# Masked products, one joining product and two loads in other slots of a fused delta-rule and gated-MLP kernel

## The chip, the cores and the metric

The kernel runs on one core of one Trainium2 chip. The metric is the device time of one launch in microseconds (us), the median of the runs shown. The engines of the core are PE (TensorE, matrix products), DVE (VectorE), ACT (ScalarE), POOL (GpSimd) and SP (SyncE, which here issues every DMA). Each runs its own instructions in the order in which they stand in the program, and a semaphore holds an instruction back until what it needs is there.

## What is computed

An attention of the delta-rule kind, token by token, whose output rows go through a gated MLP. All tensors are float32; the batch is 4, with 8 heads, 768 tokens and a head size of 48, and the MLP has the widths 384 and 1536.

```python
k_n = k / (norm(k) + 1e-06)
for t in range(S):
    y[:, :, t] = einsum('bhd,bhde->bhe', q[:, :, t], state)
    v_old = einsum('bhde,bhd->bhe', state, kt)
    state = state + bt * einsum('bhd,bhe->bhde', kt, vt - v_old)
...
x = y.transpose(0, 2, 1, 3).reshape(B * S, H * D)
gate = 1.0 / (1.0 + np.exp(-(x @ w_gate)))
return (gate * (x @ w_val)) @ w_out
```

## The kernel before

**Groups.** The 768 tokens are cut into 12 groups of 64 (g = 0 to 11), each for all 32 heads at once. Inside a group the recurrence is solved as a triangular system, and between groups the state `su` is carried. A group passes these steps, each a function of its own: `gram` (K times K, tiles pg, and copies out of it), `norms` (the keys' norms, some 18 small DVE steps), `solve` or, for groups 0 to 2, `solve_halves` (the triangular inverse `mt`, on DVE), `masked` (K times Q, tiles pp, and its product with a mask on DVE, L324, into `kqp`), `rest` (what the state already predicts, pk, subtracted on DVE as R, L456), `updates` in three steps (U of the first 32 tokens, pu, L476, copied by ACT into `su`, L482; its effect on the others, pk again, L468; U of the other 32), `rows` (the output rows yy), `advance` (the state, pd) and `flip` (transposes to the MLP's layout).

`solve_halves` inverts two 16-by-16 halves with DVE and joins them with two products on PE: pz = A times mt (L413), then a transpose of mt into `scratch` on DVE (L421) and a copy of pz on ACT (L422), then pm (L424, the second joining product), and last mt minus pm on DVE (L429). It is a generator; each `steps(halves1)` runs it to its next `yield`.

**Slots.** The MLP of a group is 12 gate tiles (gv, L557 for group 0 and L560 for the others) and 12 output products (po, L585 and L591). They stand in slots: an even slot 2i issues gate tile i, an odd one the output product of the tile two before. 24 slots are a group. The attention of group g+1 is put into the slots of group g's MLP. In `slot(s)` the order is: the gate or output product; the functions in `plan[s]`; the halves of the gated tile (ACT's sigmoid L565, DVE's product L566, and the split into high and low part, L571 and L576, from group 1 on); the functions in `late[s]`; those in `tail[s]`. So the tables `plan`, `late` and `tail` are the order, written by hand. Only the small DVE steps of `norms`, `solve` and group 2's halves are dealt out by `spread`, which gives each slot a share of room 1.6 less `busy[s]`; a masked product counts 1.4 in its slot and the next.

**Weights.** 36 pieces of 384 KB come in as raw words. `scaled(n)` (two ACT steps, L189 and L191) makes piece n usable and, when done, issues the load of piece n + 6; DVE joins the words (L203, u), and ACT and DVE split them in high and low parts (w, L212 and L219) for the groups from 1 on. SP issues these loads in order with those of the groups: `load_rows` (kv, L117, part 1 the values and part 0 the keys by token, 384 KB each), `load_q` (kqp, L109, 2 x 256 KB) and `load_k` (L105).

**Banks.** The tiles pg, pz, pm, pp, pu, yy and pt share the two PSUM banks of the tag "aux" in turn: a tile waits until what read the one before the last is done.

Of the kernel before, what the change touches and what calls it, by code (L numbers as in the profile page):

```python
# [55 lines left out]
def deltanet_gated_mlp(ctx: ExitStack, tc: tile.TileContext, kd, qd, kv, beta, words, out):  # L56
# [29 lines left out]
    def pace(ins, after):  # L86
        if after is not None:
            tc.add_manual_dep(ins.ins, after.ins.name, mybir.DependencyInfo(mybir.DependencyClass.Sync, mybir.DependencyReason.DATA), reason="pace")
# [18 lines left out]
    def load_q(g, after=None):  # L107
        for e in range(2):
            ins = nc.sync.dma_start(kqp[g % 2][64 * e:64 * e + 64, 2 + e:4 + e].rearrange("p s c t -> p (s c t)"), qd[g, e])  # L109
            pace(ins, after)  # L110

    def load_rows(g, part):

        st = state[g]
        if "kv" not in st:
            st["kv"] = wk.tile([128, 2, CP, D], F32, name=f"kv_{g}", tag="kv", bufs=2)
        nc.sync.dma_start(st["kv"][:, part].rearrange("p c d -> p (c d)"), kv[g, :, part * CP * D:(part + 1) * CP * D])  # L117
        if part:
            st["beta"] = wk.tile([128, 32], F32, name=f"beta_{g}", tag="beta", bufs=2)
            nc.sync.dma_start(st["beta"], beta[:, g])  # L120

    def load_group(g):
        load_k(g)
        load_q(g)
        load_rows(g, 1)
        load_rows(g, 0)
# [57 lines left out]
    def scaled(n):  # L184

        half, lo, hi = words_of(n)
        nc.scalar.activation(lo.bitcast(I32), half, AF.Copy, bias=-4095.5 / 8192, scale=1 / 8192)  # L189
        h = hi.bitcast(F32)  # L190
        done[n] = nc.scalar.activation(h, h, AF.Prelu, scale=2.0 ** -112, alpha=-2.0 ** 32)  # L191
        if n + BEHIND in range(EAGER, len(pieces)):
            load_piece(n + BEHIND, done[n])
# [117 lines left out]
    def masked(g):  # L311

        kq = kqp[g % 2]
        pool, tag = (ps_aux, "aux") if g else (ps_out, "po")
        pp = [pool.tile([128, J, C], F32, name=f"pp_{g}_{e}", tag=tag) for e in range(2)]
        for j in range(J):
            for e, x in KINDS:
                r, t = 64 * e, tokens_at(e, x)
                nc.tensor.matmul(out=pp[e][t:t + 64, j], lhsT=kq[r:r + D, x, j], rhs=kq[r:r + D, 3 if x else 2 + 2 * e, j], start=True, stop=True)  # L319

        def masks():
            for e, x in sorted(KINDS):
                t, sec = tokens_at(e, x), 5 if x else 2 + 2 * e
                nc.vector.tensor_tensor(out=kq[t:t + 64, sec], in0=pp[e][t:t + 64],  # L324
                                        in1=pmask[t:t + 64, e].unsqueeze(1).to_broadcast([64, J, C]), op=ALU.mult)
                yield
        return masks()
# [105 lines left out]
    def rest(g):  # L433

        st = state[g]
        kq, V = kqp[g % 2], st["kv"][:, 1]
        st["pk"] = pk = [ps_seq.tile([128, J, D], F32, name=f"pk_{g}_{e}", tag="seq") for e in range(2)]
        if g == 0:
            for e in range(2):
                nc.tensor.matmul(out=pk[e].rearrange("q j d -> q (j d)"), lhsT=flat[:, 0:128], rhs=su[:, 2].rearrange("q j d -> q (j d)").bitcast(BF16)[:, 0:J * D],  # L440
                                 start=True, stop=True, skip_group_check=True)
        for j in range(J if g else 0):
            for e, x in KINDS:
                r, t = 64 * e, tokens_at(e, x)
                nc.tensor.matmul(out=pk[e][t:t + 64, j], lhsT=kq[r:r + D, x, j], rhs=su[r:r + D, 2 if x else e, j],  # L445
                                 start=j == 0, stop=True, skip_group_check=True)
        if g == 0:
            st["R"] = [V[:, e * J:(e + 1) * J] for e in range(2)]
        else:
            st["R"] = [wk.tile([128, J, D], F32, name=f"R_{g}_{e}", tag="row", bufs=3) for e in range(2)]  # L450
            less(g)
# [61 lines left out]
    def advance(g):  # L513

        if g == N - 1:
            return
        Kt = state[g]["kv"][:, 0]
        if 1:
            pd = [ps_seq.tile([128, J, D], F32, name=f"pd_{g}_{t}", tag="seq") for t in range(2)]
            for j in range(J):  # L520
                for e, x in KINDS:
                    r, t = 64 * e, tokens_at(e, x)
                    nc.tensor.matmul(out=pd[t // 64][r:r + D, j], lhsT=Kt[t:t + 64, e * J + j], rhs=su[t:t + 64, 3 if x else e, j], start=True, stop=True)  # L523
            for e, x in KINDS:
                r, t = 64 * e, tokens_at(e, x)
                sl = su[r:r + D, 2 if x else e]
                if g == 0:
                    nc.scalar.copy(sl, pd[t // 64][r:r + D])
                else:
                    nc.vector.tensor_tensor(out=sl, in0=sl, in1=pd[t // 64][r:r + D], op=ALU.add)  # L530
# [73 lines left out]
    plan = collections.defaultdict(list)  # L604
    late = collections.defaultdict(list)

    def steps(gen, n=1):
        def fn():
            for _ in range(n):
                next(gen, None)  # L610
        return fn

    def spread(gen, total, lo, hi, room=lambda s: 1.0, into=plan):

        done, upto, whole = 0, 0.0, sum(room(s) for s in range(lo, hi))
        for s in range(lo, hi):
            upto += total * room(s) / whole
            n = total if s == hi - 1 else round(upto)
            into[s].append(steps(gen, n - done))
            done = n  # L620
# [5 lines left out]
    def take(gen, n=1):  # L626
        for _ in range(n):
            next(gen, None)
# [37 lines left out]
    halves0, norms1, halves1 = solve_halves(0), norms(1), solve_halves(1)  # L666
# [32 lines left out]
    flip(0, 1)  # L699
    busy_array(gap[0], 2)  # L700
    tail = collections.defaultdict(list)
    for n, at in enumerate((0, 0, 1, 2, 3, 5, 6, 8, 9, 9, 10, 10, 11, 12, 12, 13, 14, 15, 16, 16, 17, 18, 18), 13):
        plan[at].append(lambda n=n: scaled(n))
    spread(joins, len(pieces) - 4, 0, 20)
    for at, n in ((0, 8), (1, 4), (2, 6), (3, 4), (4, 5), (5, 5), (6, 1), (9, 1), (10, 1), (11, 1)):
        plan[at].append(steps(halves1, n))
    plan[10].append(steps(halves1))
    spread(splits, 12, 9, 24, into=tail)
    spread(splits, 3, 24, 29, into=tail)
    spread(splits, len(pieces) + 1 - 15, 29, 44, into=tail)  # L710
    for s in range(4, 8):
        tail[s].append(steps(scalings[1], 4))
    for part in (1, 0):
        plan[6].append(lambda part=part: load_rows(2, part))
    plan[8].append(lambda: load_q(2))
    halves2 = solve_halves(2)
    plan[12].append(lambda: clear(2))
    plan[23].append(lambda: joint(2))
# [4 lines left out]
    def mask_later(g, s):  # L723
        def fn():
            masks = masked(g)
            take(masks, 2)
            plan[s + 1].insert(0, steps(masks, 2))
        late[s].append(fn)
        for i in range(2):
            busy[s + i] += 1.4  # L730

    def gram_later(g, s):
        def fn():
            copies = gram(g)
            for i, n in enumerate((4, 2, 4)):
                plan[s + 1 + i].append(steps(copies, n))
        late[s].append(fn)

    solves = []
    for g in range(N):  # L740
        w = W * (g - 1)
        if g == 0:
            late[3].append(lambda: advance(0))
            continue
        up, at_rows = (13, 19) if g < 3 else (10, 16)
        at_rest = {1: 8, 2: 28}.get(g, w + 6)
        late[at_rest].append(lambda g=g: rest(g))
        for step in range(3):
            late[w + up + 2 * step].append(lambda g=g, step=step: updates(g, step))
        late[w + at_rows].append(lambda g=g: rows(g))  # L750
        late[w + at_rows].append(lambda g=g: advance(g))
        for c in range(2):
            late[w + at_rows + 2].append(lambda g=g, c=c: flip(g, c))
            busy[w + at_rows + 2] += 0.6
        busy[at_rest] += 1.1
        busy[w + up + 2] += 1.1
        busy[w + at_rows] += 1.1
        busy[w + at_rows + 1] += 1.1
        if g == 1:
            mask_later(1, 11)  # L760
        else:
            if g > 2:
                plan[w - 27].append(lambda g=g: load_group(g))
            gram_later(g, {2: 3, 3: 32}.get(g, w - 18))
            mask_later(g, w + 1 if g == 2 else w - 12)
            if g > 2:
                solves.append((g, w - 13 if g == 3 else w - 14, w + 9))
            scaling(g, {2: 25, 3: 43}.get(g, w - 7))
# [77 lines left out]
```

## Time and profile before

| | us |
|---|---|
| median of the 3 runs | 649.55 |
| lowest and highest run | 645.4, 651.54 |
| the profiled execution's own time | 646.87 |
| its span, first to last instruction | 645.2 |
| granted clock of TensorE, mean | 0.994 |

The profile is one execution. A row of its timeline has the start and the length in us, the engine, the line, the operation, the tile written and the tiles read, the shapes, how many instructions are merged in it, and in brackets how long the engine stood idle before it and what ended that. Float32 products run as two instructions each, so a row of 64 matmuls is 32 in the program. In the DMA view a queue's row has its packets, megabytes, and the time that these took as a share of 16 engines; q1 carries the loads and stores that SP issues, q8 and q14 carry instructions. A slice is a fortieth of the span, 16.1 us.

### The profile page before, as it was taken

The page shows a single profiled execution, that of the slowest core. Times are in us where ns is not written, and L with a number is a line of the kernel's source. Part 1 is how long each engine was busy: PE and PEld are TensorE (multiplying, and loading weights), DVE is VectorE, ACT ScalarE, POOL GpSimd, SP SyncE. Part 2 cuts the span into 40 slices and gives each one's busy share as a digit, 9 for nine tenths or more (in the row PEclk, how much of TensorE's full clock was granted, in tenths as well). Part 3 has the DMA queues.
Part 4 walks back from the last instruction along what each step waited for, and adds up shares of the span by engine and source line. Part 5 has one row for each costly group of instructions (what it writes and reads, how often), then busy time and mean ns, then how long its engine had stood idle before and what let it go on. Part 6 is the DMA issues. An engine that isn't in the chain of part 4 may idle for free.

```text
span 645.2 us, 24064 instructions
## 1 busy us (share of the span) xinstructions
PE 622.1 (96%) x10548; PEld 582.1 (90%) x10556; DVE 467.3 (72%) x1443; ACT 320.6 (50%) x870; POOL 11.3 (2%) x30
## 2 busy tenths in 40 slices
PE   6789799999999999999999999999999999999996
PEld 4457578889999999999999999999999999999996
DVE  5878687688987977977977977977977977952221
ACT  4879584577345346246256256256255355334222
POOL 6000000000000000000000000000000000000000
PEclk9889999999999999999999999999999999999999
DMA  9595722202103102103102112112113100100101
GB/s 267 188 295 181 230 76 84 53 2 85 38 16 84 37 16 86 28 25 84 26 27 85 25 28 85 26 28 85 25 28 85 25 4 3 25 3 3 25 1 25
DMA packets 17769, 41.07 MB, mean 64 GB/s; under 512 B 4224, under 2 KB 7296, under 8 KB 17664
## 3 DMA queue, kind: packets, MB, share of 16 engines
q1 hardware_dynamic: 17664, 39.53, 21.3%
q8 instruction: 83, 1.36, 0.9%
q14 instruction: 22, 0.18, 0.1%
HBM read 34.80 MB, written 4.72 MB: 61 GB/s over the span
## 4 chain that ended last, share of the span: by engine, by line
PE 91%; DVE 4%; ACT 2%; issue 2%; DMA 1%; ACTq 0%; SPq 0%; DVEq 0%
PE gv L560 44%; PE po L591 23%; PE gv L557 3%; PE pu L476 3%; PE yy L502 2%; PE yy L505 2%; PE po L585 2%; PE pg L291 2%; PE pp L319 2%; PE pk L445 2%; PE pd L523 2%; PE pk L468 1%; PE pt L541 1%; PE pm L408 1%; PE pz L99 1%
## 5 line engine op out<-in xcount | busy, mean ns | idle before, releaser
L560 PE MATMUL gv<-xx,w 128*128 128x256 f32 x2376 | 307.5, 283 | 0.0
L560 PEld LDWEIGHTS gv<-xx,w 128*128 128x128 f32 x2376 | 301.3, 191 | 0.9
L591 PE MATMUL po<-w,h 128*128 128x384 f32 x792 | 166.2, 345 | 0.0
L565 ACT ACTIVATE sg<-gv 128x256 f32<-128x256 f32 x144 | 55.3, 384 | 203.6 <-PE gv L560 187.2
L591 PEld LDWEIGHTS po<-w,h 128*128 128x128 f32 x792 | 133.3, 188 | 3.1
L566 DVE TENSOR_TENSOR sg<-sg,gv 128x256 f32<-128x256 f32 x144 | 60.3, 419 | 78.0 <-ACT sg L565 77.5
L571 ACT CAST h<-sg 128x256 fp32r<-128x256 f32 x132 | 53.5, 405 | 51.5 <-DVE sg L566 50.2
L350 DVE TENSOR_TENSOR X<-X,tmp 128x126 f32<-128x126 f32 (+22 forms) x279 | 71.3, 256 | 9.0
L347 DVE TENSOR_TENSOR tmp<-X,gp 128x126 f32<-128x126 f32 (+22 forms) x279 | 71.0, 254 | 7.9
L576 DVE TENSOR_TENSOR h<-sg,h 128x256 fp32r<-128x256 f32 x132 | 55.0, 417 | 28.6 <-ACT h L571 28.6
L482 ACT COPY su<-pu 32x384 f32<-32x384 f32 x92 | 43.3, 471 | 15.1 <-PE pu L476 13.9
L279 ACT ACTIVATE kv<-kv,mq 128x48 f32<-128x48 f32 x192 | 48.2, 329 | 0.0
L324 DVE TENSOR_TENSOR kqp<-pp,pmask 64x512 f32<-64x512 f32 x48 | 32.2, 686 | 7.3 <-PE pp L319 6.3
L530 DVE TENSOR_TENSOR su<-su,pd 48x384 f32<-48x384 f32 x40 | 22.1, 552 | 19.3 <-PE pd L523 18.8
L303 ACT COPY G<-pg 32x256 f32<-32x256 f32 (+1 forms) x69 | 25.4, 368 | 18.1 <-PE pg L291 16.8
L557 PE MATMUL gv<-xx,u 128*128 128x256 f32 x144 | 33.7, 385 | 0.3 <-ACT xx L544 0.3
L557 PEld LDWEIGHTS gv<-xx,u 128*128 128x128 f32 x144 | 26.6, 190 | 4.9 <-ACT xx L544 0.8
L456 DVE TENSOR_TENSOR R<-kv,pk 128x384 f32<-128x384 f32 x44 | 22.4, 550 | 1.4 <-PE pk L445 1.4
L476 PEld LDWEIGHTS pu<-R,mt 32*32 32x32 f32 x1408 | 16.5, 105 | 4.9 <-issue 1.7
L212 ACT CAST w<-u 128x384 fp32r<-128x384 f32 x36 | 18.0, 508 | 5.7 <-DVE w L219 5.6
L476 PE MATMUL pu<-R,mt 32*32 32x48 f32 x1408 | 19.4, 202 | 0.9 <-DVE kqp L324 0.9
L189 ACT ACTIVATE raw<-raw 128x384 int32<-128x384 uint16 x36 | 19.9, 553 | 0.2 <-DMA raw<-in_words_dram 0.2
(104 smaller groups left out, 515.7 us busy)
## 6 DMA issues: line engine op xcount, KB each, us to landing
raw<-in_words_dram SPq DMA_DIRECT2D x36, 384.0 KB, 5.6
kv<-in_kv_dram SPq DMA_DIRECT2D x24, 384.0 KB, 4.3
kqp<-in_qd_dram SPq DMA_DIRECT2D x24, 256.0 KB, 4.2
kqp<-in_kd_dram SPq DMA_DIRECT2D x24, 192.0 KB, 3.5
out_dram<-ot SPq DMA_DIRECT2D x48, 96.0 KB, 2.2
beta<-in_beta_dram SPq DMA_DIRECT2D x12, 16.0 KB, 4.0
```

The lines of the kernel that those rows point to most:

```text
L279: nc.scalar.activation(V[:, c], V[:, c], AF.Copy, scale=mq[:, c, 0:1])
L347: nc.vector.tensor_tensor(out=tmp, in0=X[:, k:16, j:j + 1].to_broadcast([128, n, j]), in1=gp[:, j:j + 1, 0:j].to_broadcast([128, n, j]), o ...
L350: nc.vector.tensor_tensor(out=X[:, k:16, 0:j], in0=X[:, k:16, 0:j], in1=tmp, op=ALU.add)
L476: nc.tensor.matmul(out=pu[0 if g else x][r:r + 32, j], lhsT=mt[r:r + 32, e * J + j], rhs=R[e][r:r + 32, j], start=True, stop=True)
L482: nc.scalar.copy(su[r:r + 32, 3 if x else e], pu[0][r:r + 32])
L557: nc.tensor.matmul(out=pg[:, o], lhsT=parts[w, f][:, k * 128:(k + 1) * 128], rhs=x[0][:, k], start=k == 0, stop=k == KC - 1)
L560: nc.tensor.matmul(out=pg[:, o], lhsT=parts[w, f][:, a, k * 128:(k + 1) * 128], rhs=x[b][:, k], start=(k == 0 and q == 0), stop=(k == KC - ...
L565: nc.scalar.activation(h, st["gv", f][:, 0], AF.Sigmoid)
L566: nc.vector.tensor_tensor(out=h, in0=h, in1=st["gv", f][:, 1], op=ALU.mult)
L571: nc.scalar.copy(hh[:, 0], st["sg", f])
L576: nc.vector.tensor_tensor(out=hh[:, 1], in0=st["sg", f], in1=hh[:, 0].bitcast(F32), op=ALU.subtract)
L591: nc.tensor.matmul(out=po[s], lhsT=hh[:, a, ts], rhs=parts["o", f][:, w], start=(f == 0 and q == 0), stop=(f == NF - 1 and q == 2))
```

## The change

Four things move; no instruction is added or removed, and no size changes.

1. In the table of `scaled`, pieces 22 and 24 go from slots 9 and 10 to slots 10 and 11 (the table starts at piece 13).
2. In slot 10 the transpose L421 and the copy L422 of group 1 go to the front of `plan[10]`, and the second joining product goes from `plan[10]` to `late[10]`.
3. Part 0 of group 2's rows goes from slot 6 to slot 11, and group 2's q from slot 8 to slot 13.
4. The masked product of group 1 goes from `late[11]` to `late[14]`, that of group 3 from `late[36]` to `late[38]`. U of group 1 is in `late[13]` and `late[17]`, that of group 2 in `late[37]` and `late[41]`. The masks follow in the same slot and the next, and `busy` moves with them, so `spread` deals the small DVE steps differently around those slots.

```diff
-    for n, at in enumerate((0, 0, 1, 2, 3, 5, 6, 8, 9, 9, 10, 10, 11, 12, 12, 13, 14, 15, 16, 16, 17, 18, 18), 13):
+    for n, at in enumerate((0, 0, 1, 2, 3, 5, 6, 8, 9, 10, 10, 11, 11, 12, 12, 13, 14, 15, 16, 16, 17, 18, 18), 13):
         plan[at].append(lambda n=n: scaled(n))
...
-    for at, n in ((0, 8), (1, 4), (2, 6), (3, 4), (4, 5), (5, 5), (6, 1), (9, 1), (10, 1), (11, 1)):
+    for at, n in ((0, 8), (1, 4), (2, 6), (3, 4), (4, 5), (5, 5), (6, 1), (9, 1), (11, 1)):
         plan[at].append(steps(halves1, n))
-    plan[10].append(steps(halves1))
+    plan[10].insert(0, steps(halves1))
+    late[10].append(steps(halves1))
...
-        plan[6].append(lambda part=part: load_rows(2, part))
-    plan[8].append(lambda: load_q(2))
+        plan[{1: 6, 0: 11}[part]].append(lambda part=part: load_rows(2, part))
+    plan[13].append(lambda: load_q(2))
...
-            mask_later(1, 11)
+            mask_later(1, 14)
...
-            mask_later(g, w + 1 if g == 2 else w - 12)
+            mask_later(g, {2: 25, 3: 38}.get(g, w - 12))
```

On PE, slots 10 to 14 stood like this before (pm_1 is the second joining product, pp_1 the masked product, whose 32 rows alternate between two banks; pu_1_0 is the first U, also 32 rows):

```order
L557 MATMUL gv_0_5_1189<-xx_0_781,u_7_1013 128x256 x6
L408 MATMUL pm_1_1112<-scratch_86 32x32 x64
L585 MATMUL po_0_0_979<-u_6_987,sg_0_3_1025 128x384
L585 MATMUL po_0_1_980<-u_6_987,sg_0_3_1025 128x384
L319 MATMUL pp_1_0_1293<-kqp1_77 64x64
L319 MATMUL pp_1_1_1294<-kqp1_77 64x64
...
L557 MATMUL gv_0_6_1329<-xx_0_781,u_8_1035 128x256 x3
L557 MATMUL gv_0_6_1329<-xx_0_781,u_9_1108 128x256 x3
L585 MATMUL po_0_0_979<-u_8_1035,sg_0_4_1057 128x384
L585 MATMUL po_0_1_980<-u_8_1035,sg_0_4_1057 128x384
L476 MATMUL pu_1_0_0_1370<-R_1_0_1094,mt_78 32x48
```

and now stand like this, on PE up to slot 14:

```order
L408 MATMUL pm_1_1105<-scratch_86 32x32 x64
L585 MATMUL po_0_0_979<-u_6_987,sg_0_3_1024 128x384
L585 MATMUL po_0_1_980<-u_6_987,sg_0_3_1024 128x384
L557 MATMUL gv_0_6_1294<-xx_0_781,u_8_1034 128x256 x3
L557 MATMUL gv_0_6_1294<-xx_0_781,u_9_1101 128x256 x3
L585 MATMUL po_0_0_979<-u_8_1034,sg_0_4_1054 128x384
L585 MATMUL po_0_1_980<-u_8_1034,sg_0_4_1054 128x384
L476 MATMUL pu_1_0_0_1343<-R_1_0_1091,mt_78 32x48
...
L557 MATMUL gv_0_7_1383<-xx_0_781,u_10_1199 128x256 x6
L319 MATMUL pp_1_0_1401<-kqp1_77 64x64
L319 MATMUL pp_1_1_1402<-kqp1_77 64x64
```

The masked product has passed the gate tile gv_0_6, an output product, the first U and the gate tile gv_0_7; the second joining product already stood behind gv_0_5 on PE.

On SP, the loads from group 2's values on stood in this order before (kv_2 are group 2's rows, kqp0 from in_qd its q, raw the weight pieces):

```order
L117 DMA kv_2_1016<-in_kv_dram 128x768
L120 DMA beta_2_1018<-in_beta_dram 128x32
L117 DMA kv_2_1016<-in_kv_dram 128x768
L172 DMA raw_26_1050<-in_words_dram 128x768
L109 DMA kqp0_76<-in_qd_dram 64x1024 x2
L172 DMA raw_27_1102<-in_words_dram 128x768
L172 DMA raw_28_1106<-in_words_dram 128x768
```

and on SP they are now, from the six pieces that follow beta_2 on:

```order
L120 DMA beta_2_1018<-in_beta_dram 128x32
L172 DMA raw_26_1049<-in_words_dram 128x768
L172 DMA raw_27_1099<-in_words_dram 128x768
L172 DMA raw_28_1193<-in_words_dram 128x768
L172 DMA raw_29_1197<-in_words_dram 128x768
L172 DMA raw_30_1280<-in_words_dram 128x768
L172 DMA raw_31_1284<-in_words_dram 128x768
L117 DMA kv_2_1016<-in_kv_dram 128x768
L172 DMA raw_32_1303<-in_words_dram 128x768
L172 DMA raw_33_1307<-in_words_dram 128x768
L172 DMA raw_34_1333<-in_words_dram 128x768
L109 DMA kqp0_76<-in_qd_dram 64x1024 x2
```

The keys of group 2 have passed six weight pieces and its q eight.

On DVE, slots 36 and 37 had this order before (L253 is a norm step of group 3, h_1_5 and sg_1_6 are halves of gated tiles, pp_3 the masked product of group 3):

```order
L253 SCALAR_TENSOR_TENSOR ny_3_2260<-nt_3_2261,ny_3_2260 128x32
L576 TENSOR_TENSOR h_1_5_2272<-sg_1_5_2242,h_1_5_2272 128x256
L566 TENSOR_TENSOR sg_1_6_2298<-sg_1_6_2298,gv_1_6_2277 128x256
L324 TENSOR_TENSOR kqp1_77<-pp_3_0_2301,pmask_81 64x512 x2
L219 TENSOR_TENSOR w_24_2275<-u_12_1347,w_24_2275 128x384
L219 TENSOR_TENSOR w_25_2338<-u_12_1347,w_25_2338 128x384
L324 TENSOR_TENSOR kqp1_77<-pp_3_1_2302,pmask_81 64x512 x2
```

and has this one now, on DVE in slot 36:

```order
L253 SCALAR_TENSOR_TENSOR ny_3_2260<-nt_3_2261,ny_3_2260 128x32
L249 SCALAR_TENSOR_TENSOR nt_3_2261<-ny_3_2260 128x32
L251 TENSOR_TENSOR nt_3_2261<-nt_3_2261,gp_3_2257 128x32
L253 SCALAR_TENSOR_TENSOR ny_3_2260<-nt_3_2261,ny_3_2260 128x32
L255 TENSOR_TENSOR ns_3_2262<-ny_3_2260,gp_3_2257 128x32
L576 TENSOR_TENSOR h_1_5_2272<-sg_1_5_2242,h_1_5_2272 128x256
L566 TENSOR_TENSOR sg_1_6_2302<-sg_1_6_2302,gv_1_6_2277 128x256
L219 TENSOR_TENSOR w_24_2275<-u_12_1310,w_24_2275 128x384
```

Four norm steps now stand ahead of the gated tile's halves, and the masks (L324) have gone two slots down. ACT's order in those slots is unchanged: the cast L571 of h_1_6, then the four copies L482 of U.

## The prediction

> **What bounds the kernel now.** I read the page first, for the share of each engine over the span and for the slices.
>
> ```profile
> span 645.2 us, 24064 instructions
> PE 622.1 (96%) x10548; PEld 582.1 (90%) x10556; DVE 467.3 (72%) x1443; ACT 320.6 (50%) x870; POOL 11.3 (2%) x30
> PE   6789799999999999999999999999999999999996
> q8 instruction: 83, 1.36, 0.9%
> ```
>
> TensorE (PE) works 96% of the span. From the sixth slice on each is at 90% or more, so what can be given back lies in the first five (16 us each) and, in small pieces, behind them. The view of waits, for PE alone, says what the holes are (total us, times, longest):
>
> ```profile
> PE pg L291 <- DMA kqp<-in_kd_dram: 4.3, 2, 3.8
> PE pp L319 <- issue: 2.9, 1, 2.9
> PE pu L476 <- issue: 2.5, 2, 1.5
> PE pz L99 <- DVE tmp L391: 2.3, 1, 2.3
> PE pu L476 <- DVE kqp L324: 0.9, 1, 0.9
> PE pm L408 <- issue: 0.8, 2, 0.6
> ```
>
> The first, third and fourth lie before 40 us, where the change does nothing. The change reaches the second (the masked product of group 1), the fifth (group 2's U behind group 3's masked product) and the last (the joining product pm of group 1). "issue" means that no semaphore explains the wait. The timeline of PE around the two large ones:
>
> ```profile
> 64.17 1.47 PE L408 MATMUL pz<-mt,scratch 32*32 32x32 f32 x128
> 65.57 2.86 PE L557 MATMUL gv<-xx,u 128*128 128x256 f32 x12
> 68.73 0.31 PE L408 MATMUL pm<-scratch 32*32 32x32 f32 x12 [0.30 <-DVE nt L249]
> 69.59 1.19 PE L408 MATMUL pm<-scratch 32*32 32x32 f32 x116 [0.55 <-issue]
> 70.71 1.56 PE L585 MATMUL po<-u,sg 128*128 128x384 f32 x4
> 72.20 0.34 PE L319 MATMUL pp<-kqp 48*64 48x64 f32 x7
> 75.45 1.08 PE L319 MATMUL pp<-kqp 48*64 48x64 f32 x57 [2.92 <-issue]
> 76.47 2.86 PE L557 MATMUL gv<-xx,u 128*128 128x256 f32 x12
> 79.16 1.45 PE L585 MATMUL po<-u,sg 128*128 128x384 f32 x4
> ```
>
> Both "issue" waits fall inside a run of equal matmuls, and between them lie 116 + 4 + 7 = 127. The page gives instruction queue q8 83 packets, 1.36 MB, so 16.4 KB each; PE's 10,548 + 10,556 instructions over 83 are 254, or 127 matmuls with their weight loads. So I read these waits as PE out of instructions until its next packet comes. The DMA view in three stretches, 66.7 to 66.9, then 67 to 73, then 73 to 73.1 us:
>
> ```profile
> q8 instruction: 1, 0.02, 43.2%
> ...
> q1 hardware_dynamic: 657, 1.84, 100.2%
> ...
> q8 instruction: 1, 0.02, 68.3%
> ```
>
> One packet begins at 66.8 and PE resumes at 69.59; none begins from 67 to 73 while the load queue keeps all 16 engines at 100.2%; the next begins at 73.0 and PE resumes at 75.45. From a packet's start to PE's restart it is 2.4 to 2.8 us. [...]
>
> **The change, part by part.** *The second joining product and its inputs.* On PE, pm already stood behind its slot's gate tile, so that order stays. What moves is ahead of it: the transpose L421 on DVE passes two joins, the copy L422 on ACT passes raw_22 and raw_23 (and raw_24 goes a slot later). pm waited 0.30 us for them; now both end before the gate tile does (65.57 + 2.86 = 68.43). Gain 0.30; if not, 0.
>
> *The masked product of group 1.* Its 64 matmuls leave slot 11 and come after slot 14's gate tile. PE then runs pm from 68.43 (128 matmuls, 1.24 at the rate of the 116), po (72.20 - 70.71 = 1.49), and the gate tile gv(0,6) from 71.16. The place where the packet is needed, 127 to 128 matmuls behind the twelfth of pm, becomes the eighth of gv(0,6), at 71.16 + 7 x 0.224 (2.69 us for 12, from 76.47 to 79.16) = 72.73. If the packet still let PE go at 75.45, 2.72 us of wait would stay, and 1.46 us would be gained in all: PE would have done seven gate matmuls (1.57) more by then than before, and seven of pp (0.11) less.
>
> *The loads.* What must shorten the rest is the queue of loads. SP's order before, from the timeline of its issues:
>
> ```profile
> 60.16 0.42 SPq L117 DMA_DIRECT2D kv<-in_kv_dram  x1
> 63.45 0.33 SPq L172 DMA_DIRECT2D raw<-in_words_dram  x1
> 63.82 1.11 SPq L109 DMA_DIRECT2D kqp<-in_qd_dram  x2
> 65.03 7.54 SPq L172 DMA_DIRECT2D raw<-in_words_dram  x7
> ```
>
> The kv load (384 KB) goes behind raw_31 and the two q loads (512 KB) behind raw_34, past six and eight weight pieces. 0.90 MB leave the queue ahead of the packet at 73.0. At the 1.84 MB in 6 us of the stretch above this is 2.9 us, so the packet would begin at 70.1 and PE could go on at 72.5 to 72.9, against a need at 72.73. The bounds: nothing (2.72 stays) and all. I take all, because raw_28 and raw_30 also go a slot later, and the packet before it, which cost 0.55 us, loses a kv load ahead of it too. Together the three waits are 0.30 + 0.55 + 2.92 = 3.77 us.
>
> What covers the moved work? Rows of DVE, of PE's U in slot 17, and of ACT:
>
> ```profile
> 70.83 0.69 DVE L429 TENSOR_TENSOR mt<-mt,pm 128x512 f32<-128x512 f32 x1
> 76.56 2.70 DVE L324 TENSOR_TENSOR kqp<-pp,pmask 64x512 f32<-64x512 f32 x4 [5.04 <-PE pp L319]
> 87.43 1.01 DVE L456 TENSOR_TENSOR R<-kv,pk 128x384 f32<-128x384 f32 x2
> 90.33 0.88 PE L476 MATMUL pu<-R,mt 32*32 32x48 f32 x64
> 79.36 0.38 ACT L565 ACTIVATE sg<-gv 128x256 f32<-128x256 f32 x1 [7.15 <-PE gv L557]
> ```
>
> DVE stood idle 5.04 us and ACT 7.15 us for the late PE, so both can follow an earlier PE. The new order puts the masks (2.70 us) ahead of R's second difference, for which slot 17's U waits. From L429's end (71.5) to R's end (88.4) DVE now has 11.9 us of work; with 0.6 us of norm and solve steps that come earlier and about 1.4 us of waiting for the gate of slot 14, R ends near 85.3. U would start at 90.33 - 3.77 = 86.6. About 1 us is left. pp's second bank is now the one that U used, free when four copies L482 (1.96 us) are done; a whole gate tile (2.69) lies between. Cost 0; without that cover, 1 to 2 us.
>
> *The masked product of group 3.* It goes from slot 36 behind slot 38's gate tile, so that U no longer waits for its bank.
>
> ```profile
> 135.87 1.41 PE L319 MATMUL pp<-kqp 48*64 48x64 f32 x64
> 137.21 1.32 PE L591 MATMUL po<-w,h 128*128 128x384 f32 x6
> 139.41 0.88 PE L476 MATMUL pu<-R,mt 32*32 32x48 f32 x64 [0.88 <-DVE kqp L324]
> 140.22 2.41 PE L560 MATMUL gv<-xx,w 128*128 128x256 f32 x18
> 143.62 0.58 PE L468 MATMUL pk<-su,L 32*32 32x48 f32 x35
> 137.43 0.41 DVE L566 TENSOR_TENSOR sg<-sg,gv 128x256 f32<-128x256 f32 x1
> 138.04 0.41 ACT L571 CAST h<-sg 128x256 fp32r<-128x256 f32 x1
> 140.35 1.96 ACT L482 COPY su<-pu 32x384 f32<-32x384 f32 x4 [1.91 <-PE pu L476]
> 142.71 0.22 DVE L255 TENSOR_TENSOR ns<-ny,gp 128x32 f32<-128x32 f32 x1
> ```
>
> Here something is late next. The planner fills the room with four norm steps (some 0.95 us by their spacing) ahead of DVE's sg(1,6), which then ends at 138.8 instead of 137.84. ACT's cast L571 waits for it, and the copies L482 stand behind that cast: 139.2 + 1.96 = 141.2. PE without pp and the wait does po from 135.87 (about 1.1 to the next start), U from 136.95 (0.81 to 140.22 before) and the gate tile until 140.0. pp's second bank is U's, so pp waits 1.2 us. The gain: pk started at 143.62 and would start at 140.0 + 1.2 + 1.1 + 1.1 = 143.4. I take 0.2; bounds: the whole 0.9 and the quarter that pp took over the 1.1 of group 1's, and a loss of 0.5 if the cast is later still.
>
> Sum: 3.77 + 0.2 = 3.97 us. The profiled execution took 646.87 (span 645.2 and 1.7 around it), so 642.9.
>
> **The rivals.** *The packet comes no sooner.* Gain 1.46 + 0.2: 645.2 us. For it: no view shows when a packet is asked for, which may have been at 72. [...]
>
> *The waits are no refills and stay.* Only 0.30 + 0.2 is gained: 646.4 us. Against it stands the count of 127.
>
> *A refill is late in the new dense place, and it ends slower.* Counting 128 on from gv(0,6)'s eighth, the next two packets are needed in the 44th matmul of pp and the 24th of slot 17's U; between the two places only about 6.9 us pass (the rest of pp, po, pk, the gate tile, po, a third of U), and the kv and q loads now run there. With the 2.8 us from a packet's start to PE's restart, the packet may begin 4.1 us after the first place. To end slower it must begin 4.1 + 3.97 = 8.1 us after it; the one at 73.0 began 3.4 after the wait of 69.59. The loads there (0.90 MB moved, raw_35 and the next k, 0.79 MB) are 5.5 us at the rate above, so they alone don't do it; twice that, 11 us, would wait 6.9 us and give 642.9 + 6.9 = 649.8.
>
> *More goes than this trace shows.* The runs of before spread from 645.4 to 651.54 us. If part of that is the length of these waits, other runs gain more; with the lowest run as base, 645.4 - 3.97 = 641.4.
>
> **How the numbers follow.** The three runs have the median 649.55, 2.7 above the profiled one. If those 2.7 us lie elsewhere, the median after is 649.55 - 3.97 = 645.6; if they lie in waits that go, 642.9. I forecast the middle, 644.2. Chances: the forecast 0.62, no sooner 0.17, waits stay 0.08, slower 0.04, more goes 0.09. The range goes from 641.4 to 648.0, the latter being the second case on the median run (649.55 - 1.66 = 647.9); it leaves the third and fourth on such a run outside. About 1% is what a measurement of this kernel can tell; faster by that is below 643.05: the last case and a third of the first, 0.29. Slower by 1% needs 656, which only the dense place with several late refills could give, 0.03. The rest, 0.68, is within 1%.
>
> **What would show it.** Right: no "issue" wait of PE between 60 and 90 us; a q8 packet that begins before 71 us; L319 of group 1 between slot 14's gate tile and po; a wait of pp in slot 38 on L482 of about a microsecond, and none of U in slot 37. Wrong: a wait inside gv(0,6) (loads were not what delayed the packet), one inside pp, pk or U of slots 14 to 17 (dense refills), or one of slot 17's U on L456 (masks ahead of R).

## The result and the profile after

| | before | after |
|---|---|---|
| median of the runs, us | 647.71 (11 runs) | 642.88 (11 runs) |
| lowest and highest, us | 644.94, 651.54 | 641.85, 644.45 |
| ratio of after to before, 95% interval | | 0.9928 [0.9906, 0.9949] |

The change makes the kernel 4.8 us faster, 0.7%, against a forecast of 644.2 us. One execution of the changed kernel, the first and profiled one, took 1505.85 us, with matmuls 1.4 to 2.3 times as long by shape, for a cause that no run shows; the median counts it (642.83 without), the lowest and highest leave it out, and the profile shown here is that of a second job of the same kernel (e1 below), whose own time is 642.67 us. Its page, by the same lines as before:

```profile
span 640.9 us, 24065 instructions
PE 620.9 (97%) x10548; PEld 581.4 (91%) x10556; DVE 467.3 (73%) x1443; ACT 320.7 (50%) x870; POOL 11.3 (2%) x30
PE   6789999999999999999999999999999999999996
q8 instruction: 83, 1.36, 0.9%
```

The work is the same (10,548 matmuls, 83 instruction packets), and the fifth slice has gone from 7 to 9. The view of waits, for PE (total us, times, longest):

```profile
PE pg L291 <- DMA kqp<-in_kd_dram: 4.7, 2, 4.1
PE pu L476 <- issue: 1.7, 2, 1.0
PE pz L99 <- DVE tmp L391: 1.4, 1, 1.4
PE pp L319 <- ACT su L482: 0.8, 1, 0.8
PE pm L408 <- issue: 0.7, 2, 0.5
PE gv L557 <- issue: 0.5, 1, 0.5
PE yy L502 <- ACT su L482: 0.4, 1, 0.4
```

The 2.9 us of pp on "issue" are gone, and so are the 0.9 us of pu on L324. Three waits are new: 0.5 us inside a gate tile, and two on L482, ACT's copies of U. (The waits of pu lie before 40 us, and the longer one of pm is now in group 2's pm, behind the part that was changed.) The timeline of PE in slots 10 to 17 shows the first:

```profile
66.58 1.29 PE L408 MATMUL pm<-scratch 32*32 32x32 f32 x128
67.80 1.56 PE L585 MATMUL po<-u,sg 128*128 128x384 f32 x4
69.19 1.89 PE L557 MATMUL gv<-xx,u 128*128 128x256 f32 x8
71.63 1.13 PE L557 MATMUL gv<-xx,u 128*128 128x256 f32 x4 [0.55 <-issue]
72.60 1.45 PE L585 MATMUL po<-u,sg 128*128 128x384 f32 x4
73.99 0.88 PE L476 MATMUL pu<-R,mt 32*32 32x48 f32 x64
74.80 2.86 PE L557 MATMUL gv<-xx,u 128*128 128x256 f32 x12
77.59 1.16 PE L319 MATMUL pp<-kqp 48*64 48x64 f32 x64
...
85.06 0.88 PE L476 MATMUL pu<-R,mt 32*32 32x48 f32 x64
```

pm runs through with no wait. PE stops once, behind eight matmuls of gv(0,6); to within one matmul that is where the prediction put the place at which the next packet is needed. Neither pp nor slot 17's U waits. (Group 0's first gate tile starts at 42.31 us here and at 43.90 before. This start lies between 41.65 and 44.51 us in the profiles of this study, earlier or later for kernels that are alike up to there, so times below are counted from it.)

The other two waits stand in slots 38 and 43. First PE, then ACT (e1 again):

```profile
131.93 0.88 PE L476 MATMUL pu<-R,mt 32*32 32x48 f32 x64
132.74 2.40 PE L560 MATMUL gv<-xx,w 128*128 128x256 f32 x18
135.08 0.33 PE L319 MATMUL pp<-kqp 48*64 48x64 f32 x2
136.24 1.15 PE L319 MATMUL pp<-kqp 48*64 48x64 f32 x62 [0.84 <-ACT su L482]
146.99 0.31 PE L502 MATMUL yy<-su,kqp 48*64 48x48 f32 x2
147.68 1.14 PE L502 MATMUL yy<-su,kqp 48*64 48x48 f32 x62 [0.37 <-ACT su L482]
```

```profile
133.84 0.41 ACT L571 CAST h<-sg 128x256 fp32r<-128x256 f32 x1 [0.70 <-DVE sg L566]
134.27 1.92 ACT L482 COPY su<-pu 32x384 f32<-32x384 f32 x4
145.27 0.41 ACT L571 CAST h<-sg 128x256 fp32r<-128x256 f32 x1 [1.56 <-DVE sg L566]
145.71 1.92 ACT L482 COPY su<-pu 32x384 f32<-32x384 f32 x4
```

U ends at 132.8, but its copies begin only at 134.27: ACT stands idle at the cast ahead of them, which waits for DVE. The copies end at 136.2, and pp, whose second bank they free, goes on at 136.24. The same happens 11 us later with U's other half: copies until 147.6, the row products yy from 147.68.

To see where the time went, PE's timeline is cut at four starts: group 0's first gate tile, pm of slot 10, the first state product pd (L523) behind it, and PE's matmul 2,900 (counted from 0), which lies behind slot 43. The last column is a stretch within the third part: from slot 36's gate tile, gv(1,6), to the pd that follows. The profiled executions of all kernels that are told of below (us; the rest to the last matmul was 477.2 before, 477.2 under e1 and 477.1 under e9):

| kernel | to pm | pm to pd | pd to matmul 2,900 | gv(1,6) to pd |
|---|---|---|---|---|
| before | 24.83 | 28.63 | 65.10 | 20.56 |
| after (e1) | 24.28 | 25.51 | 65.99 | 21.19 |
| after (e9) | 24.28 | 25.03 | 65.59 | 21.20 |
| e2, the loads alone | 24.85 | 28.87 | 65.01 | 20.57 |
| e3, group 1's masked product alone | 24.85 | 26.79 | 65.12 | 20.57 |
| e4, group 3's masked product alone | 24.83 | 32.01 | 65.72 | 21.19 |
| e12, after without parts 1 and 2 | 24.85 | 24.99 | 65.54 | 21.19 |
| e7, after without part 3 | 24.52 | 26.16 | 65.88 | 21.19 |
| e6 and e11, after without group 3's move | 24.28, 24.28 | 25.58, 25.46 | 64.98, 64.66 | 20.56, 20.56 |
| e5 and e10, after with the copies first | 24.28, 24.28 | 25.37, 25.75 | 63.69, 63.96 | 19.41, 19.41 |

So the change gains 0.55 us in the first part and 3.1 to 3.6 in the second, and loses 0.5 to 0.9 in the third: 2.8 to 3.7 us in all, while the medians differ by 4.8. The last column makes the third part sharper: the move of group 3's masked product costs 0.63 us in each trace that has it. What else differs there lies ahead of slot 36, above all the "issue" wait of group 2's pm (0.28 us before, 0.54 under e1, none under e9). The experiments ask which part of the change does what, whether the "issue" waits are refills, and where the rest of the 4.8 us is.

### The profile page after: what moved, and what is told of

It is laid out like the page before. It is cut to its first block, busy times and chain, and to the rows that moved or that the text cites. A ratio compares the mean times of both kernels' runs of the same rounds, so it can differ in the third digit from the quotient of the medians.

```text
span 1504.0 us, 24073 instructions
## 1 busy us (share of the span) xinstructions
PE 1494.8 (99%) x10556; PEld 1296.0 (86%) x10556; DVE 476.7 (32%) x1443; ACT 322.6 (21%) x870; POOL 11.2 (1%) x30
## 4 chain that ended last, share of the span: by engine, by line
PE 99%; DMA 0%; ACT 0%; SPq 0%; issue 0%
PE gv L560 47%; PE po L591 24%; PE gv L557 6%; PE pu L476 3%; PE po L585 3%; PE pp L319 2%; PE pg L291 2%; PE yy L505 2%; PE yy L502 2%; PE pk L445 2%; PE pt L541 1%; PE pk L468 1%; PE pd L523 1%; PE gap L99 1%; PE pz L99 1%; PE pm L408 0%
## 5 line engine op out<-in xcount | busy, mean ns | idle before, releaser
L560 PEld LDWEIGHTS gv<-xx,w 128*128 128x128 f32 x2376 | 715.0, 423 | 42.4 <-issue 23.0
L560 PE MATMUL gv<-xx,w 128*128 128x256 f32 x2376 | 735.1, 531 | 0.0
L591 PE MATMUL po<-w,h 128*128 128x384 f32 x792 | 384.8, 680 | 0.0
L591 PEld LDWEIGHTS po<-w,h 128*128 128x128 f32 x792 | 269.3, 370 | 41.3 <-issue 24.7
L557 PE MATMUL gv<-xx,u 128*128 128x256 f32 x144 | 87.8, 830 | 0.0
L557 PEld LDWEIGHTS gv<-xx,u 128*128 128x128 f32 x144 | 50.8, 358 | 32.8 <-issue 30.3
L571 ACT CAST h<-sg 128x256 fp32r<-128x256 f32 x132 | 53.3, 404 | 29.5 <-DVE sg L566 28.7
L482 ACT COPY su<-pu 32x384 f32<-32x384 f32 x92 | 43.2, 469 | 49.5 <-PE pu L476 48.3
L585 PE MATMUL po<-u,sg 128*128 128x384 f32 x48 | 45.0, 1129 | 0.0
L476 PE MATMUL pu<-R,mt 32*32 32x48 f32 x1408 | 42.3, 325 | 0.0
L324 DVE TENSOR_TENSOR kqp<-pp,pmask 64x512 f32<-64x512 f32 x48 | 32.3, 687 | 19.4 <-PE pp L319 19.0
L291 PE MATMUL pg<-kqp 48*64 48x64 f32 x768 | 32.1, 377 | 4.5 <-DMA kqp<-in_kd_dram 4.5
L291 PEld LDWEIGHTS pg<-kqp 48*64 48x64 f32 x768 | 30.4, 290 | 6.0 <-DMA kqp<-in_kd_dram 4.6
```

What stands on the lines that cost most here:

```text
L291: nc.tensor.matmul(out=pg[e][t:t + 64, j], lhsT=kq[r:r + D, x, j], rhs=kq[r:r + D, x, j], start=True, stop=True)
L476: nc.tensor.matmul(out=pu[0 if g else x][r:r + 32, j], lhsT=mt[r:r + 32, e * J + j], rhs=R[e][r:r + 32, j], start=True, stop=True)
L557: nc.tensor.matmul(out=pg[:, o], lhsT=parts[w, f][:, k * 128:(k + 1) * 128], rhs=x[0][:, k], start=k == 0, stop=k == KC - 1)
L560: nc.tensor.matmul(out=pg[:, o], lhsT=parts[w, f][:, a, k * 128:(k + 1) * 128], rhs=x[b][:, k], start=(k == 0 and q == 0), stop=(k == KC - ...
L571: nc.scalar.copy(hh[:, 0], st["sg", f])
L585: nc.tensor.matmul(out=po[s], lhsT=st["sg", f][:, s * 128:(s + 1) * 128], rhs=parts["o", f], start=f == 0, stop=f == NF - 1)
```

## The experiments

Three jobs, each with runs of the kernel before on its chip: the median of before was 647.91 us with e1 to e4 (29 runs, 644.44 to 651.74), 647.08 with e5 to e8 (14 runs) and 647.41 with e9 to e12 (11 runs). Ratios are to before.

**e1: the changed kernel once more.**

> The changed kernel as it is, for an undisturbed profile. Theory (late instruction packets): no wait of PE named issue between 60 and 90 us, a q8 packet beginning before 71 us, pp of group 3 waiting about 1.2 us in slot 38 on U's copies L482; time 4 to 5 us under the kernel before. Rival (the packet comes no sooner): a wait of 2 to 3 us inside the gate tile gv(0,6). Rival (no refills): the waits stand at the masked product of group 1, in slot 14.

Measured: 642.82 us (642.16 to 643.96), ratio 0.9918 [0.9898, 0.9939].

**e2: the loads alone, on the kernel before.**

```diff
-        plan[6].append(lambda part=part: load_rows(2, part))
-    plan[8].append(lambda: load_q(2))
+        plan[{1: 6, 0: 11}[part]].append(lambda part=part: load_rows(2, part))
+    plan[13].append(lambda: load_q(2))
```

> The kernel before with only the two loads in later slots (kv part 0 in slot 11, q in slot 13). Theory (the packet stands behind the loads): the wait of 2.92 us at the eighth pp shrinks to under 0.8 us and the 0.55 goes, so 2.5 to 3.4 us faster. Rival (loads are not what delays the packet): the wait stays at 2.5 to 3 us and the time within 0.5 us of before.

Measured: 643.76 us, ratio 0.9952 [0.9928, 0.9977]; nine of the 12 runs lie between 642.93 and 644.85, two at 648.3 and 648.5. The profiled execution took 646.38. Its PE timeline:

```profile
67.53 1.50 PE L408 MATMUL pm<-scratch 32*32 32x32 f32 x128 [0.51 <-DVE nt L249]
...
72.89 1.48 PE L319 MATMUL pp<-kqp 48*64 48x64 f32 x57 [2.09 <-issue]
74.30 4.07 PE L557 MATMUL gv<-xx,u 128*128 128x256 f32 x12
```

Of the 0.55 us inside pm no wait is listed any more (its 128 matmuls take 1.50 us here and 1.29 under e1), but of the 2.92 us 2.09 are left, where hardly 0.8 were expected. The packet began 27.8 us behind the first gate tile, and 29.1 before: 1.3 us sooner, not 2.9. And the gate tile takes 4.07 us instead of 2.86: the granted clock is 0.50 from 73.4 to 76.8 us.

**e3: group 1's masked product alone, on the kernel before.**

```diff
-            mask_later(1, 11)
+            mask_later(1, 14)
```

> The kernel before with only group 1's masked product in slot 14. Theory: the packet still begins at about 73 us, so a wait of about 2.7 us stands now inside gv(0,6), at its seventh to ninth matmul, and the time is about 1.5 us under before. Rival (no refill, something in the masked product): the wait goes to slot 14 with it or vanishes, which would give 3 us.

Measured: 644.07 us, ratio 0.9948 [0.9927, 0.997]. The profiled execution (643.65):

```profile
68.17 1.19 PE L408 MATMUL pm<-scratch 32*32 32x32 f32 x116 [0.64 <-issue]
70.68 1.89 PE L557 MATMUL gv<-xx,u 128*128 128x256 f32 x8
73.54 1.13 PE L557 MATMUL gv<-xx,u 128*128 128x256 f32 x4 [0.97 <-issue]
```

The wait stands behind the eighth matmul of gv(0,6) and is 0.97 us long, where about 2.7 were expected; pm's waits, which that figure took as gone, stay in e3 (0.29 and 0.64 us). The packet began 28.8 us behind the first gate tile, hardly sooner than before; what shrank the wait is that PE has gate matmuls to do until then, as the first rival says. From pm to pd this alone gains 1.84 us.

**e4: group 3's masked product alone, on the kernel before.**

```diff
-            mask_later(g, w + 1 if g == 2 else w - 12)
+            mask_later(g, {2: 25, 3: 38}.get(g, w - 12))
```

> The kernel before with only group 3's masked product in slot 38. Theory: U of slot 37 no longer waits, but pp waits 1 to 1.4 us on U's copies L482, which stand behind a cast that waits for DVE; 0 to 0.5 us faster. Rival (nothing takes its place): 0.9 to 1.2 us faster and no wait of PE between 133 and 145 us.

Measured: 647.93 us, ratio 1.0003 [0.9982, 1.0024]. It was expected to be up to 0.5 us faster. From pd on it loses 0.62 us, with waits of 0.83 us of pp and 0.37 of yy on L482. In the part before pd the kernel is that of before, and the profiled execution (649.64) shows there what its own did not:

```profile
70.47 0.34 PE L319 MATMUL pp<-kqp 48*64 48x64 f32 x7
74.00 1.86 PE L319 MATMUL pp<-kqp 48*64 48x64 f32 x57 [3.19 <-issue]
```

and the windows view (PE, PEld, DVE, ACT and POOL busy with their instructions, then the granted clock, DMA share, GB/s):

```profile
72.00:74.00 2.00, 0.00 (x0) 0.00 (x1) 0.00 (x0) 0.00 (x0) 0.00 (x0) 1.00 1.02 382
74.00:77.40 3.40, 3.40 (x61) 3.01 (x62) 1.56 (x3) 0.00 (x0) 0.00 (x0) 0.50 0.20 75
77.40:80.80 3.40, 3.40 (x10) 2.68 (x9) 2.26 (x5) 0.00 (x0) 0.00 (x0) 0.50 0.00 0
```

The refill wait is 3.19 us here, and behind it the clock is at 0.50 for 6.8 us, which costs about 3.4 us: 32.01 from pm to pd less 3.4 is 28.6, what the kernel before took at full clock (28.63).

**e5: the changed kernel with U's copies ahead of the cast.** For group 2's U, step 0 and step 2, the function goes from `late` to `plan`, so that ACT's copies L482 stand ahead of the cast L571 in slots 37 and 41.

```diff
-            late[w + up + 2 * step].append(lambda g=g, step=step: updates(g, step))
+            (plan if g == 2 and step != 1 else late)[w + up + 2 * step].append(lambda g=g, step=step: updates(g, step))
```

> The changed kernel with group 2's two U products issued ahead of the gated tile's cast, so that on ACT the copies L482 stand in front of L571 in slots 37 and 41; on PE the order stays. Theory (in slot 38 pp waits because L482 stands behind a cast that waits for DVE): the wait of 0.84 us of pp and that of 0.37 us of yy go, 0.8 to 1.2 us under the changed kernel, about 641.8 us. Rival (the copies are late for PE's U itself): both waits stay and the time is that of the changed kernel.

Measured: 640.95 us (639.47 to 644.63), ratio 0.9906 [0.9871, 0.9942]. Both waits on L482 are gone.

**e6: the changed kernel with group 3's masked product back in slot 36** (the edit of e4, reversed).

> The changed kernel with group 3's masked product back in slot 36. Theory (that move only trades one wait for another): within 0.5 us of the changed kernel, with a wait of about 0.9 us of U on the mask and none on L482. Rival (the move gains what it removes): 0.9 to 1.2 us slower than the changed kernel.

Measured: 641.36 us (640.97 to 642.25), ratio 0.9907 [0.9877, 0.9936]. No wait on L482, and U waits again:

```profile
133.57 0.88 PE L476 MATMUL pu<-R,mt 32*32 32x48 f32 x64 [0.87 <-DVE kqp L324]
```

The median lies 1.5 us below those of e1 and e9 on other chips, where at most 0.5 was expected. So this move, made to spare U 0.87 us, costs more than it spares: 21.19 us against 20.56 in the last column.

**e7: the changed kernel with the loads back** in slots 6 and 8 (the edit of e2, reversed).

> The changed kernel with the kv and q loads back in slots 6 and 8. Theory (the packet stands behind loads): it begins 1 to 2.5 us later than in the changed kernel, the wait in gv(0,6) grows from 0.55 to 1.5 to 2.7 us, and the time is 1 to 2 us over the changed kernel. Rival (loads don't matter): wait and time as in the changed kernel.

Measured: 643.73 us (642.63 to 645.58), ratio 0.9944 [0.9918, 0.997]. PE in slots 10 and 12:

```profile
68.77 1.19 PE L408 MATMUL pm<-scratch 32*32 32x32 f32 x116 [0.57 <-issue]
73.59 1.13 PE L557 MATMUL gv<-xx,u 128*128 128x256 f32 x4 [0.42 <-issue]
```

The wait inside pm is back, as expected, but gv(0,6) waits 0.42 us, where 1.5 to 2.7 were expected. Without the loads the rest of the change still takes away most of the long wait. Up to pd, e7 differs from e3 in parts 1 and 2 alone, and is there 0.96 us sooner (24.52 + 26.16 = 50.68 against 24.85 + 26.79 = 51.64); its packet began 27.9 us behind the first gate tile, and 28.8 in e3. So parts 1 and 2, with which raw_28 and raw_30 are issued a slot later, bring the packet sooner as well, as long as the kv and q loads stay where they were.

**e8: the kernel before with 24 small matmuls more,** issued near 12 us, long before the places in question.

```diff
-    busy_array(gap.pop(), 12)
+    early = gap.pop()
+    busy_array(early, 12)
+    for _ in range(24):
+        nc.tensor.matmul(out=early[:, 0], lhsT=flat[:, 0:128], rhs=flat[:, 0:C], start=True, stop=True)
```

> The kernel before with 24 small matmuls more near 12 us, where PE waits anyway. Theory (PE runs out of instructions every 128 matmuls): the long wait moves 24 matmuls up the program, from the eighth matmul of the masked product to about the 116th of pm, and the shorter one from the thirteenth of pm to the first of the gate tile ahead of it or goes. Rival (a wait that belongs to the masked product): it stays at its eighth matmul.

Measured: one run, 649.38 us. The PE timeline:

```profile
64.28 2.75 PE L557 MATMUL gv<-xx,u 128*128 128x256 f32 x12 [0.75 <-DVE n L244]
66.96 1.19 PE L408 MATMUL pm<-scratch 32*32 32x32 f32 x116
73.23 0.42 PE L408 MATMUL pm<-scratch 32*32 32x32 f32 x12 [5.08 <-issue]
```

Before, the long wait stood behind the seventh matmul of pp; now it stands behind the 116th of pm, 12 + 4 + 7 = 23 matmuls earlier. The shorter one stood behind the twelfth of pm, and now, 0.75 us long, it stands ahead of gv(0,5)'s first, 12 + 12 = 24 earlier (the profile puts it down to a DVE step of another group, on which no gate tile depends). Both have moved up by the 24 matmuls that were put in, to within one. A third did so too: the "issue" wait of pu at 30.6 us stands behind 59 of its 64 matmuls before and behind 35 here. Waits that move with the count of instructions and leave their tiles are read here as waits for instructions. The long one has grown to 5.08 us, since PE gets to it sooner, and the granted clock is 0.50 from 71.3, within the wait, to 78.1 us. PE stood still from 68.15 us, and the packet that let it go on began at 70.6; the DMA view from 68.2 to 70.6 has no q8 packet, and the queue of loads at

```profile
q1 hardware_dynamic: 351, 0.96, 104.0%
```

**e9 to e12: one chip for the last questions.** e9 is the changed kernel, e10 repeats e5, e11 repeats e6, and e12 is the changed kernel with parts 1 and 2 undone (pieces 22 and 24, and the joining product with its inputs, as before).

> The changed kernel once more, beside the three that follow, on the same chip: 642 to 643.5 us, 0.992 of before, with waits of about 0.5 us in gv(0,6), 0.84 of pp and 0.37 of yy on L482.

> The kernel with the copies L482 ahead of the cast in slots 37 and 41, again. Theory (both waits on L482 are paid in full on PE): 0.8 to 1.3 us under the changed kernel of this call. Rival (the gain of the earlier run was between chips): within 0.4 us of it.

> The changed kernel with group 3's masked product back in slot 36, again. Theory (the move trades a wait of 0.87 us for waits of 0.84 and 0.37): 0.1 to 0.7 us under the changed kernel of this call. Rival (the move pays): 0.3 us or more above it.

> The changed kernel with group 1's transpose L421, copy L422, second joining product and pieces 22 and 24 back in their old places. Theory (pm waits for its inputs, and the two loads issued a slot later help the packet a little): pm waits about 0.3 us again, the wait in gv(0,6) is up to 1 us longer, 0.3 to 1 us over the changed kernel of this call. Rival (this part does nothing): within 0.2 us of it.

| | us | lowest, highest | ratio, 95% |
|---|---|---|---|
| e9 | 642.89 | 641.79, 644.08 | 0.9929 [0.9913, 0.9946] |
| e10 | 640.84 | 639.59, 644.33 | 0.9904 [0.988, 0.9928] |
| e11 | 641.22 | 640.37, 643.91 | 0.9912 [0.9892, 0.9932] |
| e12 | 643.07 | 641.47, 646.21 | 0.9935 [0.9912, 0.9957] |

e10 against e9 is 2.05 us by the medians of six runs each, of which 1.63 show from pd to matmul 2,900, and 1.79 in the last column, which lies inside that part (ahead of it e10 is 0.15 us later); 0.8 to 1.3 were expected. Its rows, PE and then ACT, beside those of slots 37 and 38 above:

```profile
131.63 0.88 PE L476 MATMUL pu<-R,mt 32*32 32x48 f32 x64
132.44 2.40 PE L560 MATMUL gv<-xx,w 128*128 128x256 f32 x18
134.78 1.21 PE L319 MATMUL pp<-kqp 48*64 48x64 f32 x64
...
145.59 1.15 PE L502 MATMUL yy<-su,kqp 48*64 48x48 f32 x64
```

```profile
132.86 1.92 ACT L482 COPY su<-pu 32x384 f32<-32x384 f32 x4
134.81 0.41 ACT L571 CAST h<-sg 128x256 fp32r<-128x256 f32 x1
```

The copies begin 0.35 us behind U's end (131.63 + 0.88), 1.1 us sooner than under e1, and PE waits neither at pp nor at yy. This version is the fastest of all, 6.1 to 6.6 us below before in its two jobs; it keeps the move of group 3's masked product and takes away what made it dear. e11 is 1.67 us below e9, where 0.1 to 0.7 were expected; 0.93 of that show from pd to matmul 2,900, 0.64 of them in the last column, and the rest isn't accounted for. e12 shows pm waiting 0.50 us for its inputs again and no wait in gv(0,6); its time is 0.18 above e9, within the spread, where 0.3 to 1 were expected.

## Why the prediction was right, and where it was off

The time lay in the range, 1.3 us below the forecast. Of that, 0.5 us are the base: the forecast took 648.2 for before (644.2 + 3.97), and its median came out at 647.7. The other 0.8 are the change, forecast at 3.97 us and measured at 4.8. That the two are so near is in part luck. By PE's rows the change is worth 3.1 us: 3.73 from the first gate tile to pd, less 0.63 behind it. The other 1.5 us or so go with the clock, which the sum put at nothing; the last rival allowed for more, but by longer waits. Term by term:

**pm's inputs: 0.30 forecast, about 0.1 measured in the kernel's time.** pm itself starts 0.55 us sooner (24.83 to 24.28; in e12 24.85, with 0.50 us of waiting for the DVE step L249 ahead of it), so the wait was named rightly. But what PE gains at pm it mostly loses again in gv(0,6), where the packet is late. From the first gate tile to pd e12 takes 49.84 us, and the six profiled kernels that have the whole change up to there (e1, e9, e5, e6, e10, e11) take 49.31 to 50.03, in the mean 49.73: a difference below their spread, as is that of the medians of e12 and e9, 0.18.

**pm's inputs and the refills together: 3.77 forecast, 3.73 measured** (53.46 before, 49.73 now). That these waits are refills rests on e8, where they stand 23 and 24 matmuls earlier behind 24 matmuls more. The place of the need was right to within one matmul, behind the eighth of gv(0,6). The sum held although not all of the wait went: 0.55 us remained there under e1, 0.79 under e10, and 0.24 at most under e9 (its twelve gate matmuls take 3.10 us instead of 2.86). The brackets are short: the last matmuls ahead of a wait have long rows. Twelve matmuls of pm take 0.31 us there and seven of pp 0.34, where the 116 take 1.19 and the 57 1.08, so some 0.2 us of each wait stand in no bracket. The prediction's own two counts differ by this, 1.46 + 2.72 = 4.18 against 3.77. Slot 17's U was put at 86.6 us; by the start of group 0's first gate tile it came at 85.06 + 1.59 = 86.65.

**The share of the loads was too large.** The step "0.90 MB are 2.9 us of queue" failed: alone, the loads bring the packet 1.3 us sooner (e2), and the whole change 2.2 (it began at 69.2, 26.9 behind the first gate tile, against 29.1). The trace of before shows what was wrong in it. The kv rows, issued at 60.16 us, had landed 4.1 us later, and from 63.8 to 64.3 us the queue of loads was all but empty, so these 0.39 MB no longer stood ahead of the packet at 73.0. The DMA view from 63.8 to 64 us:

```profile
q1 hardware_dynamic: 1, 0.00, 0.3%
```

What was left ahead of it were the 0.52 MB of q, 1.7 us at the prediction's rate. No run moves q alone, and PE also came past the refill before it 0.5 us sooner in e2 (25.2 against 25.7 us behind the first gate tile), which may be a part of the 1.3. With the kv and q loads later the packet began 1.3 us sooner (e2), and in e8 no q8 packet began from 68.2 to 70.6 us, while PE stood still and the queue of loads moved 0.96 MB at 104.0%. So in these traces a backlog of loads goes with a late packet; how the DMA engines choose between the queues, no run shows.

The masked product's new place does at least as much. By PE's rows, to pd, e3 gains 1.82 us (53.46 to 51.64), where 1.46 were forecast; e2 gains 1.4 once the 1.7 us that half clock cost it are taken off (53.72 - 1.7 = 52.0); and the two together, e12, gain 3.62. There the gains add up. By the medians they don't: e3 and e2 lie 3.84 and 4.15 us below before, and the whole change 4.5 to 5.1. Each alone shortens the wait, and the clock that is lost behind a long one, as told below, can be gained only once. The prediction had the sum right, not the shares.

**Group 3's masked product: +0.2 forecast, -0.63 measured** (20.56 to 21.19 us). This is the term that was mis-sized, down to its sign. The wait of pp on L482 was named with its cause, at 1.2 us; its bracket is 0.84, but pp's third matmul starts 1.16 us behind its first (135.08 to 136.24). From slot 36's gate tile to pk the move does gain, 0.05 us (10.00 before, 133.62 to 143.62; 9.95 under e1, 128.62 to 138.57). The prediction stopped there, though: in slot 41 the same order stands once more, U's other copies behind the cast of another gated tile, and yy needs them. From yy's start to the next row product L505 it is 1.76 us under e1 (146.99 to 148.75) and 1.08 where yy does not wait, in e10 (145.59 to 146.67). The 0.68 less the 0.05 are the 0.63.

**The covers held.** U of slot 17 does not wait for R, and pp of slot 14 does not wait for its bank. No refill is late in the dense place of slots 14 to 17 beyond 0.18 us (in e6), so the slower rival did not come. That rival counted 128 matmuls from one need to the next, which no run shows to the matmul: 127 lie between the two waits of before, and e8 holds the count to within one. One of the prediction's signs of being wrong did come, a wait inside gv(0,6), small: the packet was sooner than before, but not by as much as was forecast.

**More goes than the trace shows: in part right, by the clock.** A profiled execution of before with a wait of 2.92 us kept its clock there. But e4, whose program up to there is that of before, lost 3.4 us behind one of 3.19, e2 1.7 behind one of 2.09, and e8 was at half clock behind one of 5.08. In all the changed kernels, with waits below 1 us at that place, none shows it. The runs say how much that is: each lists its mean granted clock. Of the 54 runs of before in the three jobs, 16 are below 0.993, with a median of 649.31 us; of the 22 of after (ten of the first result, e1, e9) none is. Among runs at 0.999 or more the medians are 645.28 (nine of before) and 642.18 (six of after): 3.1 us, what PE's timeline accounts for. The other 1.5 of the 4.6 between the medians of all these runs (647.40 and 642.83) go with the clock. That runs of before lose it at this wait is inferred from e4 and not shown, since only one of them was profiled. That one was at half clock elsewhere, at 20 to 23 and 37 to 40 us, and seven of the 13 profiled kernels have such a stretch before 40 us, which the change leaves alone.

What stays open: when a packet is asked for (only its start is seen), how many runs of before lose the clock at this wait, and some 0.4 to 0.8 us in the medians of e10 and e11 that PE's timeline does not show.

## What to carry to other kernels

A wait of TensorE that no semaphore explains and that falls inside a run of equal matmuls should be counted: here 127 matmuls lay between two of them, they moved up by 23 and 24 when 24 were put in ahead (e8), and the long one, 2.92 us, was shortened both by taking loads out of the queue ahead of the packet (2.09 under e2) and by putting long matmuls, not small ones, where the packet is needed (0.97 under e3). Before loads are counted as standing ahead of a packet, see whether the queue ran empty between them and it: here it did, from 63.8 to 64.3 us, and the packet came 1.3 us sooner instead of 2.9. When work is moved so that an engine need not wait for one reader, look at every other reader of the same buffers, and at what stands ahead of it on its in-order engine: here a cast that waited for DVE held back copies that were ready, in two places, and changing places with it was worth 1.8 us of PE's time. A wait can cost as much again in clock (3.4 us behind one of 3.19 under e4), so compare runs at the same granted clock before a difference is put down to the order.

## What the runs showed of the hardware

**Half clock behind short waits.** Behind waits of 2.09 us (e2) and 3.19 us (e4) the granted clock was 0.50 for 3.41 and 6.83 us, and from within one of 5.08 us (e8) for 6.83; behind one of 2.92 us (before) it stayed at 1.00. Within each of the 13 traces (before and e1 to e12) all changes of the clock lie whole steps of 3.413 us apart (in before at 19.72, 23.14, 36.79 and 40.20 us). Counted on from 40.20 us in these steps, a border falls at 74.34 and cuts the wait of before in two; that of e2 fell into one step (windows of before, before and e2, with the columns as under e4):

```profile
70.92:74.34 3.42, 1.62 (x11) 0.67 (x10) 0.59 (x1) 1.13 (x3) 0.00 (x0) 1.00 1.04 391
74.34:77.75 3.41, 2.29 (x63) 2.10 (x64) 1.18 (x2) 0.00 (x0) 0.00 (x0) 1.00 0.53 200
69.96:73.37 3.41, 1.32 (x41) 0.69 (x43) 0.32 (x1) 0.55 (x2) 0.00 (x0) 1.00 0.94 317
```

PE stood still for 1.80 and 1.12 us of the two steps in before, and the clock stayed; it stood still for 2.09 us of the one in e2, and the next step was at 0.50. In before the steps from 16.31 and 33.38 us, with 1.85 us of idle PE each, were followed by half clock too. Counted over all 13 traces, from 10 us to PE's last matmul: half clock followed each of the 8 steps at full clock with more than 1.80 us of idle PE, three of the four with 1.59 to 1.80, and none with less. So in these traces it was where a wait fell in the steps that went with its cost in clock; one of 2.92 us would put over 1.80 us into one step in about four positions of five (an estimate from the 1.80, 2.92 and 3.41 us above: 0.68 us of border positions in 3.41 leave both parts at 1.80 or less).

**From a packet to PE.** PE went on 2.2 to 2.9 us after the start of the 16-KB packet at each of 15 refill waits read for it (before, e1 to e5, e7, e8, e10 and e11). The packet itself is 0.9 to 1.4 us of that, an estimate that reads its share as the time of one engine. In the DMA view of e1, from 69.1 to 69.3 us, it takes 31.4% of 16 engines over 0.2 us:

```profile
q8 instruction: 1, 0.02, 31.4%
```

As one engine's time, 0.314 x 16 x 0.2 is 1.0 us; by this estimate the last 1.4 us before PE goes on, 1.2 to 1.6 over the 15 waits, pass with the packet already in.
